# Batch 0 of a fused attention and mixer kernel: keys transposed raw and normed by the scale of the exp, v loaded straight into place, u made by columns in PSUM, the casts of U and V planned later

## The chip, the cores and the metric

The kernel runs on one core of a Trainium2 chip. The metric is the device time of one execution in microseconds, from the runtime; the span of the profile (first to last instruction) is about 1.8 us shorter. Each run lists the mean granted clock of TensorE (1.0 is full speed). Engines: PE is TensorE, DVE VectorE, ACT ScalarE, POOL GpSimd (here it issues the loads), SP SyncE.

## The reference

```python
# q, k, v: [8, 12, 448, 64] float32, tau = 0.1; U [448, 32], V [32, 448], w_ch1 [768, 3072], w_ch2 [3072, 768]
q_n = q / (np.linalg.norm(q, axis=-1, keepdims=True) + 1e-06)
k_n = k / (np.linalg.norm(k, axis=-1, keepdims=True) + 1e-06)
scores = np.matmul(q_n, k_n.transpose(0, 1, 3, 2)) / tau
...                                     # softmax
attn_out = np.matmul(attn, v)
x = attn_out.transpose(0, 2, 1, 3).reshape(8, 448, 768)
h = x.transpose(0, 2, 1) @ U @ V        # low-rank mixing along the sequence
u = x + h.transpose(0, 2, 1)
out = u + np.maximum(u @ w_ch1, 0.0) @ w_ch2
```

Per batch there are thus 12 heads of attention, a small product with U and V, and an MLP of 768 to 3072 to 768. The MLP is most of the arithmetic.

## The kernel before

The order in which each engine issues its instructions isn't written by hand. Every instruction is an `Op` with an estimated duration, dependencies, buffers taken and given back, and a priority; a list scheduler inside the kernel simulates the engines with these estimates and fixes one order for each engine. On the chip each engine then works through its fixed order, whatever the real durations are. One of the estimates is the latency of the loads of U and V (`lat`).

```python
        ld = Slot(r_ld, 3 * (h1 - h0) // 2)
        ops = [load(lambda i=i, src=src: nc.gpsimd.dma_start(
            out=ld.tile[:, i, 0:h1 - h0, :],
            in_=src[b, h0:h1].rearrange("h (s c) d -> s h (c d)", c=SC)),
            (h1 - h0) * 0.5, acq=[ld], late=2.0 if b == 0 else LATE) for i, src in enumerate((q, k))]
        return ld, ops

...

    def load_v0(h0, h1):

        o = load(lambda: nc.gpsimd.dma_start(
            out=v_raw()[:, h0:h1, :], in_=v[0, h0:h1].rearrange("h (s c) d -> s h (c d)", c=SC)),
            (h1 - h0) * 0.5, acq=[raw])
        c = plan.add(Op("ACT/DVE", any_t(256 * (h1 - h0), 2), None, deps=[o, v0_set], prio=0.35,
                        fast=True))
        c.fn = lambda: copy_op(c, v_first()[:, h0:h1, :, 0:D],
                               v_raw()[:, h0:h1, :].rearrange("p h (c d) -> p h c d", c=SC))
        for h in range(h0, h1):
            got[0, h, "v"] = [c]
...
    # norm(): queries (i == 0) into 4 blocks, keys into 8 blocks padded with zeros, all multiplied by
    # 1/norm on DVE; then 12 transposes on PE in two groups, each copied out of PSUM by ACT or DVE
    ops = [part(1, 0), part(1, 1), part(0, 0)]
...
    # attention(), batch 0: 8 scores of 112 x 448 for a pair of heads; scale of the exp is a constant
                nc.tensor.matmul(out=sc.tile[0:rows_, 0:S], lhsT=kT[:, rows_ * m:rows_ * (m + 1)],
                                 rhs=qkT.tile[:, 8:12, :].rearrange("p c s -> p (c s)"),
                                 start=True, stop=True)
            o = plan.add(Op("PE", pe_t(S), score, deps=qdeps, acq=[sc], rel=[qkT]), pe_sc)
            exps[m] = plan.add(Op("ACT", act_t(S), lambda sc=sc, m=m: nc.scalar.activation(
                out=attn.tile[0:rows_, m, off:off + S], in_=sc.tile[0:rows_, 0:S], func=AF.Exp,
                scale=inv_tau), deps=[o], acq=[attn], rel=[sc], prio=0.1 if b == 0 else 1))
...
    # stage0(): A = U^T X (copied out), u = V^T A + X by rows, added on DVE (u_nat), then transposed
    # into uT and copied once more
...
    def cast_v():
        nc.scalar.copy(out=V_sb[:, PAD:PAD + S].rearrange("r (c s) -> r s c", c=SC),
                       in_=V_f().rearrange("r (s c) -> r s c", c=SC))
```

The comments that begin with a name and a colon stand in for cut code.

Of the kernel before, what the change touches and what calls it, by code (L numbers as in the profile page):

```python
# [20 lines left out]
PAD = 64  # L21
# [179 lines left out]
def kernel(  # L201
# [57 lines left out]
    r_inv = ring(3, [SCH, 2, G, SC], FP, "inv")  # L259
# [7 lines left out]
    VN = H * SC * D  # L267
    r_w2 = Ring(1, lambda i: pool.tile([128, VN + H * SC * (D + 2)], BF, name="raw_v", tag="w2", bufs=1)
# [6 lines left out]
    def v_raw():  # L275
        return raw.tile[0:SCH, 0:VN].rearrange("p (h e) -> p h e", h=H)

    def v_first():
        return raw.tile[0:SCH, VN:].rearrange("p (h c d) -> p h c d", h=H, c=SC)

# [15 lines left out]
    ident = const.tile([128, 128], BF, name="ident")  # L296
    w1_sb = const.tile([128, CC, F], BF, name="w1_sb")
# [16 lines left out]
    pe_tp = plan.stream("PE")  # L314
    pe_av = plan.stream("PE")
    pe_a = plan.stream("PE")
    pe_sc = plan.stream("PE")
    pe_mlp = plan.stream("PE")
# [36 lines left out]
    def flip(stream, ins, n, into, part, deps, acq, rel):  # L355
# [3 lines left out]
        for z, x in enumerate(ins):  # L359
            def fn(z=z, x=x):  # L360
                if z == 0:
                    tp.tile = psum.tile([128, len(ins), n], BF, name="tp", tag="mm", bufs=3)
                nc.tensor.transpose(out=tp.tile[:, z, :], in_=x(), identity=ident[:n, :n])  # L363
            o = plan.add(Op("PE", 0.05, fn, deps=deps + [id_set] if z == 0 else (), acq=[tp] + acq,
                            rel=rel if z == len(ins) - 1 else []), stream)
        c = plan.add(Op("ACT/DVE", any_t(n * len(ins), 2), None, deps=[o], acq=acq, rel=[tp],
# [8 lines left out]
    def load_qk(b, h0, h1):  # L375
        ld = Slot(r_ld, 3 * (h1 - h0) // 2)
        ops = [load(lambda i=i, src=src: nc.gpsimd.dma_start(  # L377
            out=ld.tile[:, i, 0:h1 - h0, :],
            in_=src[b, h0:h1].rearrange("h (s c) d -> s h (c d)", c=SC)),
            (h1 - h0) * 0.5, acq=[ld], late=2.0 if b == 0 else LATE) for i, src in enumerate((q, k))]  # L380
        return ld, ops
# [24 lines left out]
    def load_v0(h0, h1):  # L406

        o = load(lambda: nc.gpsimd.dma_start(
            out=v_raw()[:, h0:h1, :], in_=v[0, h0:h1].rearrange("h (s c) d -> s h (c d)", c=SC)),
            (h1 - h0) * 0.5, acq=[raw])  # L410
        c = plan.add(Op("ACT/DVE", any_t(256 * (h1 - h0), 2), None, deps=[o, v0_set], prio=0.35,
                        fast=True))
        c.fn = lambda: copy_op(c, v_first()[:, h0:h1, :, 0:D],
                               v_raw()[:, h0:h1, :].rearrange("p h (c d) -> p h c d", c=SC))
        for h in range(h0, h1):
            got[0, h, "v"] = [c]

    def stats(b, h0, h1, ld, ops):
# [3 lines left out]
        ss, ln, nv, inv = Slot(r_ss, 1), Slot(r_ln, 1), Slot(r_ln, 1), Slot(r_inv, 3 * g // 2)  # L422
        red = []
        for i in range(2):
            for a0 in range(0, g, G // 2):
                a1 = min(g, a0 + G // 2)
                sq = Slot(r_sq, 1)
                o = Op("ACT/DVE" if b == 0 else "DVE", any_t(256 * (a1 - a0), 2, 0.17), None,
                       deps=[ops[i]], acq=[sq], prio=pr + 0.2, fast=True)

                def square(o=o, i=i, a0=a0, a1=a1, sq=sq):
                    x, y = ld.tile[:, i, a0:a1, :], sq.tile[:, 0:a1 - a0, :]
# [18 lines left out]
        o = plan.add(Op("DVE", 0.21, lambda: nc.vector.tensor_scalar_add(  # L451
            nv.tile[:, :, 0:g, :], nv.tile[:, :, 0:g, :], EPS), deps=[o], prio=pr))
        o = plan.add(Op("DVE", 0.35, lambda: nc.vector.reciprocal(
            inv.tile[:, :, 0:g, :], nv.tile[:, :, 0:g, :]), deps=[o], acq=[inv], rel=[nv], prio=pr))
        for p in range(h0 // 2, h1 // 2):
            norm(b, p, ld, inv, 2 * p - h0, [o], pr)

    count = [0]

    def norm(b, p, ld, inv, a, deps, pr):  # L460
# [3 lines left out]
        xn, qkT = Slot(r_xn, 2 if by_pe else 1), Slot(r_qkT, 8 if b == 0 else 7)  # L464
# [31 lines left out]
    def attention(b, p, X):  # L496
        off = PAD * (b % 2)
        qkT, qdeps = got.pop((b, p, "qkT"))
# [4 lines left out]
        for m in range(8 if small else 7):  # L503
            sc = Slot(r_sc, 1)

            def score(sc=sc, m=m):
                kT = qkT.tile[:, 0:8, :].rearrange("p b s -> p (b s)")
                nc.tensor.matmul(out=sc.tile[0:rows_, 0:S], lhsT=kT[:, rows_ * m:rows_ * (m + 1)],  # L508
                                 rhs=qkT.tile[:, 8:12, :].rearrange("p c s -> p (c s)"),
# [324 lines left out]
```

## Time and profile before

| | before |
|---|---|
| time, median of 4 runs | 612.28 us (612.0 to 612.3) |
| span of the profile | 610.5 us |
| first exp of batch 0 | 16.59 us |
| last exp of batch 0 ends | 44.92 us |
| first matmul of the MLP of batch 0 | 48.05 us |
| transposes of batch 1 | 61.05 us |

The lines of the page and the timeline that carry this are in the prediction below. From the first MLP matmul on, PE is dense. So two numbers say almost everything of a version of this kernel: when the MLP starts, and how much of PE's time after that isn't work. I call the second slack: the length of a stretch minus the matmuls in it, each counted by the step at which it follows its neighbour in dense rows (0.1625 us for 384 columns, 0.2155 for 512, 0.19 for a score, 0.032 for an av matmul, 0.05 for a transpose of 112). In the kernel before, the slack is 0.6 us from 60 to 80 us, 1.5 from 80 to 160, and within the error of the count after that, up to the start of the last matmul (3.8 us before the end, in before and after alike).

### The profile page before, as it was taken

Reading aid. Unit: us, or ns where it says so; the run is one execution under the profiler, and the core shown is the slowest. Engines: PE = TensorE matmul, PEld = TensorE weight load, DVE = VectorE, ACT = ScalarE, POOL = GpSimd, SP = SyncE. Lnnn points to the kernel's source line nnn. Section 1 sums busy time; section 2 is a strip of 40 time slices with the busy share of each in tenths; the row PEclk is TensorE's granted clock in tenths of the full one; section 3 lists DMA queues with packets and bytes.
Section 4 is the critical chain, followed back from the end, with each engine's and each line's share of the span. In section 5 each row is a group of like instructions: output and inputs, shape, how many; then the busy total and the mean of one; then the engine's idle time right before and its main releaser. Section 6 shows DMA issues by size and latency. Waiting matters only on the chain.

```text
span 610.5 us, 11561 instructions
## 1 busy us (share of the span) xinstructions
PE 585.5 (96%) x4704; PEld 348.3 (57%) x4728; DVE 298.6 (49%) x758; ACT 285.0 (47%) x609; POOL 109.9 (18%) x168
## 2 busy tenths in 40 slices
PE   0899999999999999999999999999999999999997
PEld 0565666555555665666445666666545666654465
DVE  6977859989999799654820253014300210110011
ACT  4984981288774187407642067505542015014300
POOL 6227160135340627000600000000000000000000
PEclk9999999999999999999999999999999999999999
DMA  9999992999999999644962132031002110410011
GB/s 136 202 204 136 210 156 23 166 138 138 132 125 155 139 185 159 94 84 83 121 37 53 53 72 59 1 84 35 14 1 52 52 40 1 79 52 1 0 53 53
DMA packets 146037, 54.58 MB, mean 89 GB/s; under 512 B 109568, under 2 KB 145984, under 8 KB 145984
## 3 DMA queue, kind: packets, MB, share of 16 engines
q0 software_dynamic: 69216, 25.96, 37.9%
q1 hardware_dynamic: 76704, 27.86, 24.5%
q8 instruction: 37, 0.61, 0.4%
q14 instruction: 16, 0.13, 0.1%
q10 hardware_dynamic: 64, 0.02, 0.0%
HBM read 52.25 MB, written 11.01 MB: 104 GB/s over the span
## 4 chain that ended last, share of the span: by engine, by line
PE 91%; ACT 4%; DVE 2%; SPq 1%; DMA 1%; issue 1%; ACTq 0%
PE mm L670 36%; PE mm L649 35%; PE sc L508 9%; PE av L526 7%; ACT attn L512 3%; PE mm L587 1%; DMA raw_uv<-in_moe_U_dram 1%; PE tp L363 1%; SPq L733 1%; PE mm L559 1%; DVE ss L440 1%; ACT qkT L700 0%; ACT sq L434 0%; ACT uT L700 0%; SPq L763 0%
## 5 line engine op out<-in xcount | busy, mean ns | idle before, releaser
L649 PE MATMUL mm<-uT,w_sb 128*128 128x384 bf16 (+1 forms) x1130 | 235.4, 352 | 0.9
L670 PE MATMUL mm<-w_sb,relu 128*128 128x384 bf16 (+1 forms) x1368 | 233.7, 323 | 0.3 <-ACT uT L700 0.3
L512 ACT ACTIVATE attn<-sc 128x448 bf16<-128x448 f32 (+1 forms) x342 | 165.1, 557 | 91.4 <-PE av L526 57.6
L670 PEld LDWEIGHTS <-relu 128*128 128x128 bf16 x1368 | 132.5, 98 | 87.1 <-issue 1.3
L649 PEld LDWEIGHTS <-w_sb 128*128 128x128 bf16 x1152 | 112.2, 98 | 101.1 <-issue 0.2
L659 ACT ACTIVATE relu<-mm 128x384 bf16<-128x384 f32 (+1 forms) x174 | 95.0, 546 | 150.4 <-PE mm L649 148.6
L679 DVE TENSOR_TENSOR O_sb<-mm,u_nat 128x384 f32<-128x384 f32 (+1 forms) x57 | 31.1, 549 | 231.1 <-PE mm L670 227.6
L508 PE MATMUL sc<-qkT 128*128 128x448 bf16 (+1 forms) x342 | 103.5, 359 | 7.8 <-DVE qkT L702 4.1
L526 PEld LDWEIGHTS <-attn 128*128 128x128 bf16 (+1 forms) x1536 | 61.1, 98 | 16.1 <-issue 2.2
L399 POOL DMA_DIRECT2D v_nat<-in_v_dram x98 | 63.3, 651 | 21.2 <-DMA w_sb<-in_moe_w_ch_dram 5.3
L440 DVE TENSOR_REDUCE ss<-sq 112x8 f32<-112x512 bf16 x96 | 62.9, 672 | 0.5 <-ACT sq L434 0.3
L526 PE MATMUL av<-v_nat,attn 128*128 128x65 bf16 x1344 | 55.6, 193 | 0.0
L377 POOL DMA_DIRECT2D qk_nat<-in_q_dram x25 | 17.8, 713 | 172.3 <-DVE xn L474 115.9
L508 PEld LDWEIGHTS <-qkT 128*128 128x128 bf16 (+1 forms) x342 | 31.3, 104 | 26.0 <-issue 5.8
L535 DVE TENSOR_TENSOR X_sb<-av,rd 128x256 bf16<-128x256 f32 x96 | 40.2, 419 | 1.6
L477 DVE TENSOR_TENSOR xn<-qk_nat,inv 112x256 bf16<-112x256 bf16 x96 | 36.8, 415 | 1.9 <-DMA qkT<-xn 1.8
L533 DVE RECIPROCAL rd<-av 128x4 f32<-128x4 f32 x96 | 17.0, 179 | 34.7 <-PE av L526 33.6
L436 DVE TENSOR_TENSOR sq<-qk_nat 112x512 bf16<-112x512 bf16 x85 | 32.8, 412 | 0.0
L474 DVE TENSOR_TENSOR xn<-qk_nat,inv 112x512 bf16<-112x512 bf16 x48 | 32.6, 680 | 0.0
L601 DVE TENSOR_TENSOR u_nat<-mm,X_sb 128x384 bf16<-128x384 f32 (+2 forms) x45 | 22.4, 527 | 12.7 <-PE mm L587 12.0
L363 PE MATMUL tp<-ident,xn 112*128 112x112 bf16 x144 | 11.2, 226 | 10.4 <-DVE xn L477 10.4
L445 ACT ACTIVATE ln<-ss 112x32 f32<-112x32 f32 (+1 forms) x25 | 6.2, 248 | 31.9 <-DVE ss L440 31.9
(51 smaller groups left out, 175.4 us busy)
## 6 DMA issues: line engine op xcount, KB each, us to landing
qk_nat<-in_q_dram POOLq DMA_DIRECT2D x23, 224.0 KB, 5.7
qk_nat<-in_k_dram POOLq DMA_DIRECT2D x23, 224.0 KB, 6.8
w_sb<-in_moe_w_ch_dram POOLq DMA_DIRECT2D x4, 1152.0 KB, 18.7
w_sb<-in_moe_w_ch_dram POOLq DMA_DIRECT2D x8, 576.0 KB, 14.1
out_dram<-O_sb SPq DMA_DIRECT2D x15, 168.0 KB, 2.2
out_dram<-O_sb SPq DMA_DIRECT2D x16, 144.0 KB, 2.1
out_dram<-O_sb SPq DMA_DIRECT2D x16, 120.0 KB, 1.9
out_dram<-O_sb SPq DMA_DIRECT2D x16, 96.0 KB, 2.2
```

What stands on the lines that cost most here:

```text
L399: nc.gpsimd.dma_start(out=vb[p0:p0 + s1 - s0, hs, j, 0:D], in_=v[b, hs].rearrange("h (s c) d -> c s h d", c=SC)[c, s0:s1]),
L436: nc.vector.tensor_mul(y, x, x)
L440: lambda i=i, a0=a0, a1=a1, sq=sq: nc.vector.reduce_sum(ss.tile[:, i, a0:a1, :].rearrange("p h c -> p (h c)"), sq.tile[:, 0:a1 - a0, :].re ...
L474: nc.vector.tensor_mul(dst, src, sc.to_broadcast([SCH, 2, SC, D]))
L477: nc.vector.tensor_mul(dst, src[:, hh], sc[:, hh].to_broadcast([SCH, SC, D]))
L508: nc.tensor.matmul(out=sc.tile[0:rows_, 0:S], lhsT=kT[:, rows_ * m:rows_ * (m + 1)], rhs=qkT.tile[:, 8:12, :].rearrange("p c s -> p (c s)" ...
L512: exps[m] = plan.add(Op("ACT", act_t(S), lambda sc=sc, m=m: nc.scalar.activation(out=attn.tile[0:rows_, m, off:off + S], in_=sc.tile[0:row ...
L526: nc.tensor.matmul(out=av.tile[:, t, 0:D + 1], lhsT=attn.tile[0:rows_, m, 128 * t:128 * (t + 1)], rhs=vv[0:rows_, h, j, 0:D + 1], start=(j ...
L535: muls.append(plan.add(Op("DVE", dve_t(256), lambda av=av, rd=rd, h=h: nc.vector.tensor_mul(X.tile[:, :, h * D:(h + 1) * D], av.tile[:, :, ...
L649: o = plan.add(Op("PE", pe_t(n), lambda f=f, cc=cc, mm=mm: nc.tensor.matmul(out=mm.tile[:, 0:n], lhsT=w1_sb[:, cc, f * 128:(f + 1) * 128], ...
L659: nc.scalar.activation(out=relu.tile[:, f, 0:n], in_=mm.tile[:, 0:n], func=AF.Relu)
L670: nc.tensor.matmul(out=mm.tile[:, 0:c1 - c0], lhsT=relu.tile[:, f, i * 128:(i + 1) * 128], rhs=w2.tile[:, f, c0:c1], start=(f == 0), stop= ...
```

## The change

The intent is to take work off the path that leads to the first MLP matmul. Keys of batch 0 are transposed as loaded; their norm is multiplied in by the exp, whose scale becomes a per-partition pointer. So that a score has one head's keys in its rows, the queries carry the zero padding (8 blocks) and the keys have 4. tau goes into the norms through a small tile. v is loaded straight into its place by 12 loads in runs of 64 elements, in place of 2 loads and 2 copies. u comes by columns: X is brought in by identity matmuls and V·A added in the same PSUM bank, so one copy makes uT; u by rows is made later. The casts of U and V are planned with a latency of 12 us instead of 2.5, and V's cast writes contiguously. With these come smaller moves: the squares of the later pairs and nearly all copies of batch 0's keys and queries go to DVE, the loads of batch 0 are split and ordered anew, and its scores and the late u by rows get their own place in PE's order.

The core of the diff (ring sizes, renames and the fills of the tau tile are cut):

```diff
+        ops = [load(lambda c=c: nc.gpsimd.dma_start(
+            out=v_first()[:, h0:h1, c, 0:D],
+            in_=v[0, h0:h1].rearrange("h (s c) d -> c s h d", c=SC)[c]),
+            (h1 - h0) * 0.22, deps=[v0_set], acq=[raw]) for c in range(SC)]
...
+    def norm_q(p, ld, ops, la, inv, a, o, pr):
+
+
+        xn, qkT = Slot(r_xn, 1), Slot(r_qkT, 8)
+        EV = "DVE" if p else "ACT/DVE"
+        done = [flip(pe_tp, [(lambda c=c, hh=hh: ld.tile[:, 1, la + hh, c * D:(c + 1) * D])
+                             for c in range(SC) for hh in range(2)],
+                     SCH, lambda: qkT.tile, (lambda t_, x: (t_[:, 8:12, :], x)), [ops[1]], [qkT], [ld], 2, EV)]
+        us = []
+        for hh in range(2):
+            def unit(hh=hh):
+                src = ld.tile[:, 0, la + hh, :].rearrange("p (c d) -> p c d", d=D)
+                nc.vector.tensor_mul(xn.tile[:, 4 * hh:4 * hh + 4, 64 * hh:64 * hh + 64], src,
+                                     inv.tile[:, 0, a + hh, :].unsqueeze(2).to_broadcast([SCH, SC, D]))
+            us.append(plan.add(Op("DVE", dve_t(256), unit, deps=[o, xn_set[count[0] % len(xn_t)]], acq=[xn],
+                                  rel=[ld, inv] if hh else [], prio=pr)))
+        count[0] += 1
+        done.append(flip(pe_tp, [(lambda z=z: xn.tile[:, z, :]) for z in range(8)], SCH,
+                         lambda: qkT.tile, (lambda t_, x: (t_[:, 0:8, :], x)), us, [qkT], [xn], 1, EV))
+        got[0, p, "qkT"] = (qkT, done, inv, a)
...
+                x = qkT.tile
+                if small:
+                    kT, qT = x[:, 8 + m % 4, :], x[:, m // 4 * 4:m // 4 * 4 + 4, :]
+                else:
+                    kT = x[:, 0:8, :].rearrange("p b s -> p (b s)")[:, 128 * m:128 * (m + 1)]
+                    qT = x[:, 8:12, :]
+                nc.tensor.matmul(out=sc.tile[0:rows_, 0:S], lhsT=kT, rhs=qT.rearrange("p c s -> p (c s)"),
                                  start=True, stop=True)
-            o = plan.add(Op("PE", pe_t(S), score, deps=qdeps, acq=[sc], rel=[qkT]), pe_sc)
-            exps[m] = plan.add(Op("ACT", act_t(S), lambda sc=sc, m=m: nc.scalar.activation(
-                out=attn.tile[0:rows_, m, off:off + S], in_=sc.tile[0:rows_, 0:S], func=AF.Exp,
-                scale=inv_tau), deps=[o], acq=[attn], rel=[sc], prio=0.1 if b == 0 else 1))
+
+            def exp(sc=sc, m=m):
+                scale = inv_tau
+                if small:
+                    inv, a = keys
+                    scale = inv.tile[:, 1, a + m // 4, m % 4:m % 4 + 1]
+                nc.scalar.activation(out=attn.tile[0:rows_, m, off:off + S], in_=sc.tile[0:rows_, 0:S],
+                                     func=AF.Exp, scale=scale)
+            o = plan.add(Op("PE", pe_t(S), score, deps=qdeps, acq=[sc], rel=[qkT]), pe_first if small else pe_sc)
+            exps[m] = plan.add(Op("ACT", act_t(S), exp, deps=[o], acq=[attn],
+                                  rel=[sc] + keys[:1], prio=0.1 if b == 0 else 1))
...
+    def columns(X, A, uT, muls, cc, a):
+
+        c0 = 128 * cc
+        mm = Slot(r_mm, 1)
+        st = pe_a if cc < CC - 1 else pe_av
+        X.uses += 1
+        X.left += 1
+        A.uses += 1
+        A.left += 1
+        for t in range(3):
+            plan.add(Op("PE", 0.055, lambda t=t: nc.tensor.matmul(
+                out=mm.tile[:, 128 * t:128 * (t + 1)], lhsT=X.tile[:, t, c0:c0 + 128], rhs=ident,
+                start=(t == 0), stop=False, skip_group_check=True),
+                deps=muls[2 * cc:2 * cc + 2] + [id_set] if t == 0 else (), acq=[mm, uT] if t == 0 else [],
+                rel=[X] if t == 2 else []), st)
+        o = plan.add(Op("PE", pe_t(384), lambda: nc.tensor.matmul(
+            out=mm.tile[:, 0:384], lhsT=A.tile[:, c0:c0 + 128], rhs=V_sb[:, PAD:PAD + 384],
+            start=False, stop=True, skip_group_check=True), deps=[a], rel=[A]), st)
+        c = plan.add(Op("ACT/DVE", any_t(384), None, deps=[o], rel=[mm], prio=0))
+        c.fn = lambda: copy_op(c, uT.tile[:, cc, 0:384], mm.tile[:, 0:384])
+        return c
...
-                    deps=[zf], prio=-2, lat=2.5)))
+                    deps=[zf], prio=-2, lat=12.0)))
...
-        nc.scalar.copy(out=V_sb[:, PAD:PAD + S].rearrange("r (c s) -> r s c", c=SC),
-                       in_=V_f().rearrange("r (s c) -> r s c", c=SC))
+        nc.scalar.copy(out=V_sb[:, PAD:PAD + S].rearrange("r (c s) -> r c s", c=SC),
+                       in_=V_f().rearrange("r (s c) -> r c s", c=SC))
```

## The prediction

> **What bounds the kernel now.** I read the page first, for which engine is full and when.
>
> ```profile
> span 610.5 us, 11561 instructions
> PE 585.5 (96%) x4704; PEld 348.3 (57%) x4728; DVE 298.6 (49%) x758; ACT 285.0 (47%) x609; POOL 109.9 (18%) x168
> PE   0899999999999999999999999999999999999997
> ACT  4984981288774187407642067505542015014300
> ```
>
> PE is full in all slices but the first two and the last; ACT and DVE are full only early. So after the start the kernel is bound by PE, and a change to batch 0 can gain only in the first slices. The timeline (start, duration, engine, line, tile, count) shows what happens there:
>
> ```profile
> 10.41 1.49 PE L363 MATMUL tp<-ident,xn 112*128 112x112 bf16 x12 [10.41 <-DVE xn L477]
> 11.39 2.18 ACT L742 CAST V_sb<-raw_uv 128x448 bf16<-128x448 f32 x1 [1.73 <-DMA raw_uv<-in_moe_V_dram]
> ...
> 16.02 1.28 PE L508 MATMUL sc<-qkT 128*112 128x448 bf16 x3 [4.12 <-DVE qkT L702]
> ...
> 16.59 1.41 ACT L512 ACTIVATE attn<-sc 112x448 bf16<-112x448 f32 x3
> ...
> 30.41 3.69 ACT L512 ACTIVATE attn<-sc 112x448 bf16<-112x448 f32 x8
> ...
> 43.51 1.41 ACT L512 ACTIVATE attn<-sc 112x448 bf16<-112x448 f32 x3 [0.77 <-PE sc L508]
> ...
> 48.05 13.16 PE L649 MATMUL mm<-uT,w_sb 128*128 128x384 bf16 x80
> ```
>
> PE does nothing for 10.4 us, transposes, then waits 4.1 us, because ACT stood at the cast of V (1.7 us for its transfer, 2.2 us of work, then 0.6 us for a transfer of U) with the logarithm of the second norm behind it. From 16.59 to 44.92 ACT runs the 48 exps of batch 0 among 5 squares, 4 copies of keys or queries, norms and copies of A. Table of windows: between 16 and 45 us ACT is busy 27.63 of 29.00. After the last exp 3.1 us of tail lead to the first MLP matmul at 48.05.
>
> From there on I ask how much of PE's time is real work. In dense rows the starts lie 0.1625 us apart for 384 columns (80 matmuls in 13.16), 0.19 for a score, 0.032 for an av matmul, 0.05 for a transpose, 0.2155 for 512 columns. Counts by these steps give about 552 us of work in the 562.4 us from 48.05 to the end: 10 us of slack, of which about 3 lie at the very end, and 2.6 between 61 and 121 us. So the end moves with the start of the MLP of batch 0, minus whatever new holes appear on PE.
>
> **What the Trainium skill says.**
> "TensorE: Matmul & The Clock Gate", Back-to-back issue gap: N/2.4 + 2.5 ns for an isolated warm gap, which makes 162.5 ns for 384 columns. The trace agrees (0.1625 us). The 326 ns that the groups show for one such matmul is latency, which "Perfetto Trace Analysis", Identifying the Most-Contended Engine, warns of: busy time of matmuls is a poor measure. Hence the count above.
> "ScalarE: Activation LUTs", What ACT_TABLE_LOAD costs: an ACTIVATE with immediate scale and bias takes 186 ns + 0.833 ns per element, each per-partition pointer operand adds about 93 ns, neighbours overlap by about 93 ns. For 448 that is 559 alone and 466 apart; the trace has 540 alone and 440 to 450 apart (eight in 3.69 us). The exps of before thus cost as those with immediates. After the change their scale is a pointer into the norms; no run yet shows what that costs here.
> "DMA: Bandwidth & Descriptors", Why small descriptors are slow: a fixed cost per packet and per descriptor. The trace agrees in direction: 12 to 48 us moves up to 214 GB/s, while the loads of v in runs of 64 elements at 48 to 52 us move 88.
>
> **The change part by part.**
>
> *Start.* Keys are transposed raw, so only queries wait for the norm. But the order listing shows DVE doing four sums (both pairs) before the first reciprocal. The fills of DVE end at 7.15 now, two small ones for tau are added: 7.3. Four sums, partly waiting for squares on ACT: to 10.0. Scale 0.17, reciprocal 0.25: 10.5. Two query products at 0.38: 11.3. Eight transposes on a PE that has just begun: 12.0. Copy of 896 by ACT, 0.85: 12.9. Score: first exp about 13.4, against 16.59. Most of these 3.2 us come from the casts of U and V, which are planned with a latency of 12 us instead of 2.5 and now stand after the 16th exp at the latest, where their data has long landed.
>
> *ACT through batch 0.* It loses the 5 squares in this stretch (DVE does them), the 4 copies, and the copy of v (1.29, ahead of the first exp). It keeps 48 exps: 47 steps of 0.44 is 21; with an estimated 0.093 each from the skill's page for the pointer, 4.5 more. Two pairs of ln and exp for norms 0.9, casts of U 0.6, cast of V about 1.0 (its order is changed to contiguous writes; 2.2 before). Sum 28.0. I add 0.9 for a hole between the third and fourth exp, where PE's order has 16 transposes. The last exp ends near 42.3, against 44.92.
>
> *DVE.* Per pair it saves the query product of 0.60 and a copy of v, and takes over squares and all copies of keys and queries but two. Walking its order with the steps of the trace (sum 0.59, product 0.34, copy 0.53 or 0.30, square 0.34) has the third pair's queries ready at 24.3 and the fifth's at 32; ACT reaches them at about 24.6 and 33.5. Close, but ACT stays the slower.
>
> *Tail.* u by columns: the identity matmuls that bring X in can run early; after A only a 384-column matmul and one copy remain instead of product, add, transposes, copy. Saves about 0.5 of 3.1. The MLP starts at 42.3 + 2.6 = 44.9: **3.1 us earlier**.
>
> *PE's added work* lies before this and beside ACT: 16 half or whole transposes per pair instead of 12, 18 identity matmuls for 18 transposes, six matmuls of 384 more: 6 x (4 x 0.05) + 6 x 0.16 = 2.2 us, hidden.
>
> *After.* The order of before puts 80 MLP matmuls, then transposes of batch 1, then its scores with MLP matmuls between all of them. The order of after puts 140 (22.8 us) ahead, so the transposes of batch 1 stand at 44.9 + 22.8 = 67.7 (61.05 now), and the fill is used up: 2 scores, 12 transposes, 10 scores, 12, 2, 12, 2 follow nearly bare. There ACT sets the pace: 14 exps, three copies of 896 at 0.85, norms 1.0. Walking it, from the first transpose to the second av group takes 15 us, with 10.6 us of PE work in it: a **new hole of about 4.2 us**. Against it, the 2.6 us of slack that before has between 61 and 121 are partly filled, since 72 matmuls of the second layer are spread over the rest of batch 1 and 38 of the next MLP come ahead of batch 2: give back 1.5.
>
> Sum: 612.3 - 3.1 + 4.2 - 1.5 = 611.9. If the pointer scale costs nothing, the start moves by another 4 us (607.9). I give that one chance in four, and come to **610.9**.
>
> **The rivals.**
> (1) The early start is kept whole. For it: the plan itself sees 60 more MLP matmuls before batch 1, 9.75 us. Then the second hole eats 2 to 4 of them: 603 to 606. Against it: the plan's exps are 0.427 us, the trace has 0.44 to 0.45, and the pointer isn't in the plan at all.
> (2) Transfers become the bound. v of batch 0 is now 12 loads in runs of 64 elements (two before); at 88 GB/s its 0.69 MB take 7.8 us instead of 3.3. In the trace the first-layer weights land up to 25.8 us after issue, the last at 41.5, and the second-layer ones at 80. All would move by 2 to 4 us. But the last first-layer piece is needed only at 62, and the second layer begins at about 78 with pieces that landed from 61 on. I expect nothing; if a queue wait appears, 614 to 617.
> (3) DVE becomes the bound of batch 0 with the squares it takes over. ACT would then show holes waiting for scores: 1 to 3 us later, 612 to 614.
>
> **Range and chances.** The start is uncertain by 2 us (pointer, cast of V, holes), the hole after it by 1.5, the give-back by 1: together about 2.8, and 1.3 times that, 3.7, on each side: 607.0 to 614.5. A gain of 2% needs 600.0, more than the whole wait before 16 us could return after the hole: 0.02. A loss of 2% needs 624.5: 0.02. Within: 0.96.
>
> **What would show it.** First exp at 13 to 14 us; steps between exps of batch 0 of 0.53 instead of 0.44; the first MLP matmul at 43.5 to 46; 140 MLP matmuls with no gap; then PE waiting for exps and copies between about 67 and 80 us; second-layer matmuls waiting for no transfer. I am wrong if exps keep 0.44 apart and the MLP starts before 42, or if the weights hold PE up.

## More of the kernel before

One pair of rows of before is needed for comparison later. Timeline of DVE before the norms of batch 1 (start, duration, engine, line, operation and tiles, count, and in brackets the idle time before it with what ended it):

```profile
52.91 0.68 DVE L440 TENSOR_REDUCE ss<-sq 112x8 f32<-112x512 bf16 x1
56.95 0.24 DVE L451 TENSOR_SCALAR ln<-ln 112x32 f32<-112x32 f32 x1 [3.37 <-ACT ln L448]
```

DVE has the sums of batch 1's squares and waits 3.37 us for the logarithm, which stands in ACT's order behind the relus of the MLP.

## The result

The changed kernel takes 613.88 us (median of 4 runs, 613.85 to 614.49) against 612.28. The ratio is 1.003, with a 95% interval of 1.0012 to 1.0047. The result is correct.

So it is slower by 1.6 us, where 1.4 faster had been predicted; both lie within 2%, and 613.88 lies within the range.

The page of the kernel after, same lines as those of before in the prediction:

```profile
span 612.7 us, 11615 instructions
PE 590.0 (96%) x4732; PEld 350.2 (57%) x4755; DVE 294.4 (48%) x755; ACT 286.2 (47%) x605; POOL 116.5 (19%) x178
PE   3899899999999999999999999999999999999997
ACT  4985764277874487407742067505542014114300
```

One slice is 15.3 us. The first digit of PE rose from 0 to 3: PE starts earlier. But the fifth digit is now 8 instead of 9: something is lost between 61 and 77 us.

The start. Timeline of ACT after:

```profile
13.20 1.68 ACT L552 ACTIVATE attn<-sc,inv 112x448 bf16<-112x448 f32 x3 [0.62 <-PE sc L544]
15.76 3.25 ACT L552 ACTIVATE attn<-sc,inv 112x448 bf16<-112x448 f32 x6 [0.88 <-PE sc L544]
...
22.93 1.07 ACT L813 CAST V_sb<-raw_uv 128x448 bf16<-128x448 f32 x1
...
31.83 10.07 ACT L552 ACTIVATE attn<-sc,inv 112x448 bf16<-112x448 f32 x19 [0.27 <-PE sc L544]
```

The first exp comes at 13.20 instead of 16.59, V is cast in 1.07 us at 22.93 instead of 2.18 at 11.39, and the last of the 48 exps ends at 31.83 + 10.07 = 41.90 instead of 44.92. Three exps take 1.68 us, where the three of before took 1.41: the pointer costs 0.09 each.

What follows. Timeline of PE after:

```profile
45.03 22.91 PE L720 MATMUL mm<-uT,w_sb 128*128 128x384 bf16 x140
67.78 0.56 PE L364 MATMUL tp<-ident,xn 112*128 112x112 bf16 x8
...
69.77 0.54 PE L544 MATMUL sc<-qkT 128*128 128x448 bf16 x2 [0.58 <-ACT qkT L771]
70.15 0.75 PE L364 MATMUL tp<-ident,xn 112*128 112x112 bf16 x12
...
72.26 3.57 PE L544 MATMUL sc<-qkT 128*128 128x448 bf16 x8 [0.98 <-ACT attn L552]
75.62 1.32 PE L364 MATMUL tp<-ident,xn 112*128 112x112 bf16 x12
```

The MLP starts 3.0 us earlier. 140 matmuls run without a gap, and then there is nothing to put between the scores of batch 1: eight of them take 3.57 us, 0.43 apart instead of 0.19, because each waits for a buffer that an exp gives back. Between 67.78 and 82.23 the steps above give 9.5 us of work in 14.45: some 4.9 lost (4.6 in the count of the table below).

Why do 140 matmuls stand ahead of batch 1? Timelines of ACT and DVE after, at the norms of batch 1:

```profile
50.69 0.68 DVE L440 TENSOR_REDUCE ss<-sq 112x8 f32<-112x512 bf16 x1
63.69 0.18 DVE L454 TENSOR_SCALAR ln<-ln 112x32 f32<-112x32 f32 x1 [12.31 <-ACT ln L448]
```

```profile
62.78 0.49 ACT L730 ACTIVATE relu<-mm 128x384 bf16<-128x384 f32 x1 [0.48 <-PE mm L720]
63.17 0.22 ACT L445 ACTIVATE ln<-ss 112x32 f32<-112x32 f32 x1
63.42 0.23 ACT L448 ACTIVATE ln<-ln 112x32 f32<-112x32 f32 x1
```

The squares and sums of batch 1 are done early, so its data was there. But DVE then stands for 12.31 us (3.37 before), since ACT has the logarithm behind a row of relus that are paced by the MLP, 0.975 us apart. The chip wasn't late; the plan's estimate of the loads of batch 1 was.

A last reading from the table of windows of after (columns: stretch, its length; busy time and count of PE, PEld, DVE, ACT, POOL; then granted clock, DMA share, GB/s):

```profile
65.00:70.00 5.00, 4.42 (x37) 2.83 (x35) 4.23 (x10) 3.04 (x6) 1.45 (x2) 1.00 1.16 210
70.00:75.00 5.00, 3.60 (x23) 1.51 (x22) 5.00 (x14) 4.84 (x12) 0.00 (x0) 0.95 1.16 210
75.00:80.00 5.00, 5.00 (x64) 3.72 (x63) 3.10 (x9) 4.60 (x11) 1.40 (x2) 0.71 1.16 210
```

In this run the clock was cut to half behind the thin stretch, for 3.4 us from 74.5 us on (a window from 74.52 to 77.92 shows 0.50; the 0.95 and 0.71 above are means over 5 us). The twelve transposes at 75.62 take 1.32 us, those at 70.15 only 0.75. The three other runs of this kernel have a mean clock of 1.0 and spans of 612.1, so the cut probably cost 0.6 us of the 4.6.

### The profile page after: what moved, and what is told of

The parts are those of the page before. It is cut to its first block, busy times and chain, and to the rows that moved or that the text cites. A ratio compares the mean times of both kernels' runs of the same rounds, so it can differ in the third digit from the quotient of the medians.

```text
span 612.7 us, 11615 instructions
## 1 busy us (share of the span) xinstructions
PE 590.0 (96%) x4732; PEld 350.2 (57%) x4755; DVE 294.4 (48%) x755; ACT 286.2 (47%) x605; POOL 116.5 (19%) x178
## 4 chain that ended last, share of the span: by engine, by line
PE 91%; DVE 4%; ACT 4%; issue 1%; ACTq 0%
PE mm L720 35%; PE mm L741 34%; PE sc L544 10%; PE av L568 7%; ACT attn L552 3%; PE tp L364 1%; PE mm L657 1%; DVE ss L440 1%; PE mm L625 1%; DVE u_nat L671 1%; ACT qkT L771 1%; DVE O_sb L750 0%; DVE xn L482 0%; DVE xn L776 0%; DVE xn L508 0%
## 5 line engine op out<-in xcount | busy, mean ns | idle before, releaser
L741 PE MATMUL mm<-w_sb,relu 128*128 128x384 bf16 (+1 forms) x1368 | 238.0, 323 | 0.2 <-DVE O_sb L750 0.2
L720 PE MATMUL mm<-uT,w_sb 128*128 128x384 bf16 (+1 forms) x1130 | 228.5, 352 | 0.8
L552 ACT ACTIVATE attn<-sc 128x448 bf16<-128x448 f32 x294 | 140.9, 550 | 81.2 <-PE av L568 51.5
L730 ACT ACTIVATE relu<-mm 128x384 bf16<-128x384 f32 (+1 forms) x179 | 97.3, 544 | 154.4 <-PE mm L720 154.3
L436 DVE TENSOR_TENSOR sq<-qk_nat 112x512 bf16<-112x512 bf16 x92 | 35.6, 413 | 0.0
L508 DVE TENSOR_TENSOR xn<-qk_nat,inv 112x256 bf16<-112x256 bf16 x84 | 32.5, 412 | 0.4 <-DMA qkT<-xn 0.3
L505 DVE TENSOR_TENSOR xn<-qk_nat,inv 112x512 bf16<-112x512 bf16 x42 | 28.8, 686 | 0.0
L552 ACT ACTIVATE attn<-sc,inv 112x448 bf16<-112x448 f32 x48 | 26.3, 675 | 2.0 <-PE sc L544 2.0
L671 DVE TENSOR_TENSOR u_nat<-mm,X_sb 128x384 bf16<-128x384 f32 x36 | 19.2, 551 | 10.0 <-PE mm L657 10.0
L380 POOL DMA_DIRECT2D qk_nat<-in_k_dram x25 | 17.6, 703 | 2.1 <-PE sc L544 2.0
```

The source lines that it names most:

```text
L380: ops = [load(lambda i=i, src=src: nc.gpsimd.dma_start(out=ld.tile[:, i, lo:lo + h1 - h0, :], in_=src[b, h0:h1].rearrange("h (s c) d -> s ...
L436: nc.vector.tensor_mul(y, x, x)
L508: nc.vector.tensor_mul(dst, src[:, hh], sc[:, hh].to_broadcast([SCH, SC, D]))
L552: nc.scalar.activation(out=attn.tile[0:rows_, m, off:off + S], in_=sc.tile[0:rows_, 0:S], func=AF.Exp, scale=scale)
L720: o = plan.add(Op("PE", pe_t(n), lambda f=f, cc=cc, mm=mm: nc.tensor.matmul(out=mm.tile[:, 0:n], lhsT=w1_sb[:, cc, f * 128:(f + 1) * 128], ...
L730: nc.scalar.activation(out=relu.tile[:, f, 0:n], in_=mm.tile[:, 0:n], func=AF.Relu)
```

## The experiments

Twelve kernels ran, each in five rounds beside the kernel before (e34 has six runs, e6 four). The runs of before that each group shares have medians of 612.26, 612.17, 612.33 and 612.26. This table has all of it. "Ahead" is the number of MLP matmuls of batch 0 that stand in PE's order before the transposes of batch 1; "start" is the first MLP matmul; the slacks are as defined above; all from the profiled run of each kernel.

| kernel | ahead | start | slack 60-80 | slack 80-160 | start + slack | span | span minus that | median us |
|---|---|---|---|---|---|---|---|---|
| before | 80 | 48.05 | 0.6 | 1.5 | 50.2 | 610.5 | 560.3 | 612.28 |
| after | 140 | 45.03 | 4.6 | 3.2 | 52.8 | 612.7 | 559.9 | 613.88 |
| e1_imm (wrong result) | 140 | 42.70 | 3.9 | 2.9 | 49.5 | 610.2 | 560.7 | 612.07 |
| e2_late | 103 | 45.03 | 0.7 | 2.9 | 48.6 | 608.8 | 560.2 | 610.60 |
| e12_both (wrong result) | 103 | 43.38 | 0.8 | 2.7 | 46.9 | 607.1 | 560.2 | 608.67 |
| e3_casts | 72 | 46.60 | -0.1 | 1.7 | 48.2 | 608.8 | 560.6 | 610.10 |
| e34_casts_late | 36 | 46.11 | 0.0 | 3.2 | 49.4 | 609.3 | 559.9 | 611.96 |
| e25_vraw_late | 62 | 46.81 | 0.8 | 2.2 | 49.8 | 610.1 | 560.3 | 611.95 |
| e5_vraw | 99 | 46.68 | 0.3 | 2.5 | 49.5 | 610.4 | 560.9 | 612.22 |
| e6_nocol | 121 | 46.87 | 0.8 | 7.0 | 54.6 | 616.9 | 562.3 | 617.59 |
| e7_normed | 132 | 44.02 | 2.7 | 3.0 | 49.7 | 610.3 | 560.6 | 612.26 |
| e7_normed_late | 95 | 44.26 | 1.1 | 1.9 | 47.3 | 607.8 | 560.5 | 609.41 |
| e4_before_late | 45 | 48.15 | 0.4 | 4.7 | 53.2 | 613.4 | 560.2 | 615.18 |
| e8_half | 121 | 45.07 | 2.1 | 3.3 | 50.5 | 610.7 | 560.2 | 612.44 |

The second column from the right is the test of the reading: for 13 of 14 kernels the span is 560.4 us plus the start plus the slack from 60 to 160 us, within 0.5. So the start and the slack explain the times, and nothing else of that size does. The one that falls out, e6, lost 1.4 us between 46.87 and 60, ahead of the stretch counted, to 3.4 us at half clock (its 121 matmuls take 21.10 us from the first start to the next row, where 121 x 0.1625 is 19.66).

Read differences between kernels here, not single slacks. A recount from the same traces gives 0.2 to 0.4 us more from 60 to 80 and 0.8 to 1.4 us more from 80 to 160 in every kernel, since steps of some small matmuls have to be chosen and some records are missing. It moves the constant to 558.4 to 559.4 (561.0 in e6). PE's work after the start is 553.4 to 553.8 us in all fourteen.

My theory after the first comparison: the start gained 3 us as predicted; the place of batch 1 in the order, set by a wrong estimate of its loads, makes the hole; the pointer scale eats part of what raw keys save. Rivals: a hole set by the exps and copies of batch 1 whatever the order; the 12 short-run loads of v; and u by columns.

### e1_imm: the exps of batch 0 with a constant scale

Wrong: the keys' norms are replaced by one number.

```diff
-                    scale = inv.tile[:, 1, a + m // 4, m % 4:m % 4 + 1]
+                    scale = inv_tau / 0.8
```

> The changed kernel with the scale of the 48 exps of batch 0 as one number (10/0.8, wrong on purpose: keys are then not normed) instead of a pointer to the norms; order of instructions unchanged. My theory: the pointer costs about 0.085 us per exp and ACT is the bound of batch 0. Then exps lie 0.44 apart instead of 0.525, the first MLP matmul moves from 45.0 to 41.0 to 42.5 us, the 140 matmuls and the hole behind them stay as they are, and the time falls from 613.9 to 610 to 611.5. Rival: DVE or PE set the pace of batch 0 and ACT would only wait more; MLP start above 44, time above 613.

Measured: relative error 0.0945; 612.07 us (612.0 to 612.97), ratio to before 1.0005 (0.9993 to 1.0018). Timeline of ACT in e1:

```profile
13.20 1.41 ACT L552 ACTIVATE attn<-sc 112x448 bf16<-112x448 f32 x3 [0.62 <-PE sc L544]
15.76 2.71 ACT L552 ACTIVATE attn<-sc 112x448 bf16<-112x448 f32 x6 [1.15 <-PE sc L544]
...
23.77 2.28 ACT L552 ACTIVATE attn<-sc 112x448 bf16<-112x448 f32 x5 [0.73 <-PE sc L544]
...
30.36 8.77 ACT L552 ACTIVATE attn<-sc 112x448 bf16<-112x448 f32 x19 [0.54 <-PE sc L544]
```

The order is that of the changed kernel, so rows can be compared one to one: 1.68 against 1.41 for three, 3.25 against 2.71 for six, 10.07 against 8.77 for nineteen. The pointer costs 0.09, 0.09 and 0.07 us an exp, some 3.8 us over 48. The MLP start moved by 2.3 of these (42.70): the waits for scores grew (1.15 from 0.88, 0.73 from 0.21, 0.54 from 0.27), because PE and DVE can't feed a faster ACT. That start is just later than the theory's 42.5 at most, and the time misses 611.5 by 0.6: 1.8 us gained over the changed kernel. The hole stayed, at 3.9.

### e2_late: keys and queries of batch 1 planned 6 us earlier

```diff
-            (h1 - h0) * 0.5, acq=[ld], late=2.0 if b == 0 else LATE) for i, src in enumerate((q, k))]
+            (h1 - h0) * 0.5, acq=[ld], late=2.0 if b < 2 else LATE) for i, src in enumerate((q, k))]
```

The work stays the same; the plan's order changes, and with it the engine of two jobs that ACT or DVE may take (605 and 755 instructions in the changed kernel, 603 and 757 in e2).

> The changed kernel with one number of its plan changed: queries and keys of batch 1 are planned to land 6 us earlier, so that the order puts 103 instead of 140 MLP matmuls ahead of their transposes and fills the scores with the rest. My theory: the order, not the data, makes the hole; MLP start stays at 45.0, transposes of batch 1 at about 62, the 4.6 us of lost PE time after them fall below 1.5, time 609.5 to 611.5. Rival: the plan was right and the data is late; PE or DVE waits for a transfer and the time stays at 613 or more.

Measured: correct, 610.6 us (610.55 to 610.87), ratio to before 0.9976 (0.9964 to 0.9989). Timeline of PE in e2:

```profile
45.03 16.90 PE L720 MATMUL mm<-uT,w_sb 128*128 128x384 bf16 x103
61.77 0.56 PE L364 MATMUL tp<-ident,xn 112*128 112x112 bf16 x8
...
66.77 0.35 PE L544 MATMUL sc<-qkT 128*128 128x448 bf16 x1
66.96 0.49 PE L720 MATMUL mm<-uT,w_sb 128*128 128x384 bf16 x2
```

Same start to the hundredth, and the hole is gone (0.7 us): between the scores there are MLP matmuls again. One estimate is worth 3.3 us. The norms of batch 1 were ready in time for the earlier place, so the rival that exps and copies make the hole whatever the order falls too.

### e12_both: the two together

The edits of e1 and e2, so wrong.

> Both edits together (wrong on purpose as the first). If both costs are real and separate they add: MLP start at 41 to 42.5 and no hole, 606.5 to 608.5. If the hole only moves with the start (the data of batch 1 lands near 46 us whatever PE does), less: 609 to 610.5.

Measured: 608.67 us (608.24 to 608.91), ratio 0.9944 (0.9931 to 0.9956), just above the range. The MLP starts at 43.38, past the 41 to 42.5 expected and not at 42.70 as in e1: the plan is another one. The parts nearly add (1.8 and 3.3 alone, 5.2 together).

### e3_casts: only the casts, in the kernel before

```diff
-                    deps=[zf], prio=-2, lat=2.5)))
+                    deps=[zf], prio=-2, lat=12.0)))
...
-                      acq=[uv], prio=-2, lat=2.5)) for t in range(4)]
+                      acq=[uv], prio=-2, lat=12.0)) for t in range(4)]
...
-        nc.scalar.copy(out=V_sb[:, PAD:PAD + S].rearrange("r (c s) -> r s c", c=SC),
-                       in_=V_f().rearrange("r (s c) -> r s c", c=SC))
+        nc.scalar.copy(out=V_sb[:, PAD:PAD + S].rearrange("r (c s) -> r c s", c=SC),
+                       in_=V_f().rearrange("r (s c) -> r c s", c=SC))
...
-              plan.add(Op("ACT", 0.5, cast_v, deps=v0 + [z], rel=[uv], prio=3)),
+              plan.add(Op("ACT", 1.0, cast_v, deps=v0 + [z], rel=[uv], prio=3)),
```

> The kernel before with only the casts of U and V changed as in the change (planned for 12 us instead of 2.5, V written contiguously). My theory: most of the earlier first exp comes from these casts; first exp at 13.3 to 14.2 instead of 16.6, then ACT still has its squares and copies, MLP start at 46 to 47.2, time 610.5 to 612. Rival: the raw keys bring the start; then the first exp stays above 15 and the time at 612.3.

Measured: correct, 610.1 us (609.88 to 610.68), ratio 0.9968 (0.9955 to 0.9982). Timeline of ACT in e3:

```profile
13.18 1.41 ACT L512 ACTIVATE attn<-sc 112x448 bf16<-112x448 f32 x3 [0.37 <-PE sc L508]
...
21.54 1.06 ACT L742 CAST V_sb<-raw_uv 128x448 bf16<-128x448 f32 x1
```

Slightly better than expected. The casts alone bring the first exp from 16.59 to 13.18; the whole change brings it no further (13.20). Two edits are in this run, the later place and the contiguous writes. V's cast now stands behind the first exp, at 21.54, so its faster write (1.06 us instead of 2.18) can't be what brought that exp forward; what it gives later wasn't tried alone. Of the 3.4 us, 1.45 arrive at the MLP start (46.60), since ACT still has its squares and copies. And with 72 matmuls ahead there is no hole, so this small part of the change beats both the kernel before (by 2.2 us) and the whole change (by 3.8).

### e34_casts_late: both planning edits in the kernel before

The edits of e3 and of e2.

> The kernel before with the casts of e3 and with keys and queries of batch 1 planned 6 us earlier as in e2; correct result. Its order puts 36 matmuls of the MLP ahead of the transposes of batch 1 (72 in e3). Theory (the place of batch 1 relative to the MLP decides whether there is a hole, and e3 has none at 72 matmuls): moving batch 1 still earlier gains nothing more; the time stays at 609.5 to 610.8, MLP start 46 to 47. Rival (every microsecond of earlier batch 1 helps, because more MLP matmuls are left to fill the waits of batch 2 and later): 608 to 609.3. Against both: if 36 matmuls are too few to cover the logarithm, norms and copies of batch 1, a hole of 1 to 2 us appears before its first transposes, 611 to 612.

Measured: correct, 611.96 us (611.16 to 614.31), ratio 1.0006 (0.9991 to 1.0022). The theory said 609.5 to 610.8, so this missed. The start moved on to 46.11, but the slack after 80 us rose from 1.7 to 3.2. With only 36 matmuls ahead of batch 1, the MLP's later matmuls are spent among the scores, and waits appear further on (argued; the slack wasn't traced wait by wait). The time lies in the range of the third forecast, but the hole that it named, ahead of the first transposes, isn't there: the 36 matmuls run from 46.11 to 52.05 without one. The six runs also spread with the clock: spans of 609.4 and 609.6 at a mean clock of 1.0, 610.7 at 0.996, 611.7 at 0.994, 612.5 at 0.993. At full clock e34 is 1.3 us slower than e3 (608.1), not 1.9.

### e4_before_late: the planning edit alone, in the kernel before

The edit of e2.

> The kernel before with keys and queries of batch 1 planned 6 us earlier and nothing else; correct result; 45 matmuls ahead of the transposes of batch 1 instead of 80. Control: before has no hole there (0.6 us of slack between 60 and 80 us), so the planning alone has nothing to give. Theory: 612 to 614, as e34 against e3 (1.9 us slower by the medians). Rival (the planning helps by itself, and e2 owes its gain to it rather than to the hole of the changed kernel): 610.5 or less.

Measured: correct, 615.18 us (614.81 to 615.28), ratio 1.0044 (1.0031 to 1.0057). The direction is the theory's, the size above its range: 2.9 us slower. The slack from 80 to 160 us went from 1.5 to 4.7. More than half of that rise is one wait behind the tail of batch 1. Timeline of PE in e4:

```profile
120.58 0.35 PE L508 MATMUL sc<-qkT 128*128 128x448 bf16 x1 [1.67 <-ACT attn L512]
```

So planning batch 1 early isn't good in itself; it is good where too many MLP matmuls stood ahead, bad where there were about enough. The rival (e2 owes its gain to the planning alone) is refuted.

### e8_half: half of e2's shift

```diff
-            (h1 - h0) * 0.5, acq=[ld], late=2.0 if b == 0 else LATE) for i, src in enumerate((q, k))]
+            (h1 - h0) * 0.5, acq=[ld], late=2.0 if b == 0 else 5.0 if b == 1 else LATE) for i, src in enumerate((q, k))]
```

> The changed kernel with keys and queries of batch 1 planned 3 us earlier, half of what e2 does; correct result. 121 matmuls ahead of the transposes of batch 1 (140 in the changed kernel, 103 in e2). Theory (the hole grows with the fill that was used up before it): MLP start 45.03 as in both, slack on PE from 60 to 80 us between their 4.6 and 0.7, at 1.5 to 3.0; time between 610.9 and 612.8. Rival (a threshold: any fill left among the first scores closes the hole): slack under 1.0 and time as e2, 610.3 to 610.9. Rival (e2 gained from something else than the place of batch 1): 613 or more.

Measured: correct, 612.44 us (612.43 to 612.74), ratio 1.0003 (0.9989 to 1.0016). Ahead 103, 121, 140: slack from 60 to 80 us 0.7, 2.1, 4.6; time 610.6, 612.44, 613.88. The start was the same within 0.04 us. That is a dose and its response, inside the theory's ranges: in this plan the hole grows with the fill used up ahead of it. The count ahead doesn't fix it for every plan: e6 below also has 121, and a slack of 0.8.

### e5_vraw and e25_vraw_late: v loaded whole and copied

```diff
-        ops = [load(lambda c=c: nc.gpsimd.dma_start(
-            out=v_first()[:, h0:h1, c, 0:D],
-            in_=v[0, h0:h1].rearrange("h (s c) d -> c s h d", c=SC)[c]),
-            (h1 - h0) * 0.22, deps=[v0_set], acq=[raw]) for c in range(SC)]
-        for h in range(h0, h1):
-            got[0, h, "v"] = ops
+        o = load(lambda: nc.gpsimd.dma_start(
+            out=v_raw()[:, h0:h1, :], in_=v[0, h0:h1].rearrange("h (s c) d -> s h (c d)", c=SC)),
+            (h1 - h0) * 0.5, acq=[raw])
+        c = plan.add(Op("ACT/DVE", any_t(256 * (h1 - h0), 2), None, deps=[o, v0_set], prio=0.35,
+                        fast=True))
+        c.fn = lambda: copy_op(c, v_first()[:, h0:h1, :, 0:D],
+                               v_raw()[:, h0:h1, :].rearrange("p h (c d) -> p h c d", c=SC))
+        for h in range(h0, h1):
+            got[0, h, "v"] = [c]
```

> The changed kernel with v of batch 0 loaded whole in 3 loads and copied into place, as before, and nothing else changed; correct result. Its order puts 99 matmuls ahead of the transposes of batch 1 (140 in the changed kernel). Theory (the hole after the fill is the cost): the transposes of batch 1 stand near 61 to 62, the hole shrinks from 4.6 to under 1.5 us, time 610 to 611.5. Rival (the hole is made by the copies and exps of batch 1 themselves and stays whatever the order): 613 to 614.5.

> The changed kernel with the planning of e2 and with v of batch 0 loaded whole in 3 loads and copied into place, as before; correct result. 62 matmuls of the MLP stand ahead of the transposes of batch 1 (140 in the changed kernel, 103 in e2). Theory (order decides, the loads of v in short runs cost nothing that ends up on the path): as e2, 610.0 to 611.2, MLP start 44.5 to 46.0 because three copies of v return to DVE or ACT. Rival 2 of the prediction (the 12 short-run loads of v push later transfers): e25 is faster than e2 by 1 us or more, 608 to 609.5.

Measured: e5 is correct at 612.22 us (612.07 to 612.49), ratio 1.0002 (0.999 to 1.0013); e25 is correct at 611.95 us (611.71 to 612.2), ratio 0.9996 (0.9984 to 1.0008). Timeline of ACT in e5:

```profile
23.81 1.13 ACT L778 COPY raw_v<-raw_v 112x1024 bf16<-112x1024 bf16 x1
...
30.86 12.69 ACT L559 ACTIVATE attn<-sc,inv 112x448 bf16<-112x448 f32 x24 [0.37 <-PE sc L551]
```

A copy of v is back on ACT, and the last exp ends at 43.55, 1.65 us later than in the changed kernel; the MLP start follows (46.68). The hole shrinks to 0.3 us because the new plan puts 99 matmuls ahead, not 140. For e5 the hole part of the theory held (under 1.5), while the time is 0.7 us above its range, and e25 is 0.8 us above its range in start and in time: I had not counted on the later start. e25 against e2 (62 and 103 ahead, both without a hole) is 1.35 us slower (1.1 between their runs at full clock, spans of 609.9 and 608.8). So v straight into place gains 1.65 to 1.8 us at the start. As a whole e5 is 1.7 us faster than the changed kernel, but by its other order: the hole fell by 4.3. Where neither has a hole, the kernel without the short-run loads is the slower one, so the rival that forecast e25 at 1 us or more below e2 is refuted.

### e6_nocol: u as before

```diff
-            if b == 0:
-                ut += [columns(X, A, uT, muls, cc, a) for cc in range(c0 // 128, c1 // 128)]
...
-        late = b == 0
+        late = False
```

(The buffer count and the priority of the adds go back with it.)

> The changed kernel with u made as before (product, add, transposes, copy) and nothing else undone; correct result. 121 matmuls ahead of the transposes of batch 1. Theory: the tail to the MLP is longer by the predicted 0.5 us, so the MLP starts at 45.4 to 46.0 instead of 45.03; the hole is 19 matmuls (3.1 us) earlier and smaller, 2 to 4 us; and the 12 products of V and A that the change adds late are gone from PE (about 1.5 us). Time 611 to 613. Rival (u by columns pays more than 0.5 us): MLP start after 46.5 and time 614 or more.

Measured: correct, 617.59 us (616.97 to 618.67), ratio 1.009 (1.0077 to 1.0103). The theory missed: both numbers of the rival hold (MLP start after 46.5, 614 or more), and the hole from 60 to 80 us, expected at 2 to 4, is 0.8. From the last exp to the MLP start it takes 4.68 us (42.19 to 46.87) instead of 3.13 in the changed kernel. But that is half of the loss at most. The rest is a hole of another place. Timeline of PE in e6:

```profile
120.51 0.24 PE L625 MATMUL sc<-X_sb,U_sb 128*32 128x128 bf16 x4 [0.57 <-ACT attn L552]
...
123.10 0.23 PE L655 MATMUL sc<-A_sb,V_sb 128*128 128x128 bf16 x1 [0.46 <-DVE u_nat L666]
124.13 0.55 PE L544 MATMUL sc<-qkT 128*128 128x448 bf16 x2 [0.81 <-DVE u_nat L669]
```

The tail of batch 1 (u by rows) and the scores of batch 2 follow each other with no second-layer matmul left to fill: 5.2 us of slack between 120 and 140. Its four timed runs have clocks of 0.994 to 0.997, and the profile shows two cuts to half clock of 3.4 us, from 46.35 and from 124.86 us, each in or just behind a stretch where PE has holes (0.66 and 0.67 as means over 5 us). So undoing one part re-plans a place 70 us further on. e6 shows that u by columns isn't where the time went; what it is worth by itself can't be read from its total.

### e7_normed and e7_normed_late: raw keys undone

e7 is the changed kernel with keys and queries of batch 0 normed before the transposes, as before, and a constant scale; e7_normed_late has the edit of e2 in addition.

```diff
-            if b == 0:
-                norm_q(p, ld, ops, lo + 2 * p - h0, inv, 2 * p - h0, o, pr)
-            else:
-                norm(b, p, ld, inv, 2 * p - h0, [o], pr)
+            norm(b, p, ld, inv, 2 * p - h0, [o], pr, lo)
...
-                if small:
-                    inv, a = keys
-                    scale = inv.tile[:, 1, a + m // 4, m % 4:m % 4 + 1]
```

> The changed kernel with its first part undone and nothing else: keys and queries of batch 0 both normed before the transposes, exps with an immediate scale; v straight into place, u by columns and the later casts stay. Correct result. 132 matmuls stand ahead of the transposes of batch 1 (140 in the changed kernel). By subtraction of the runs so far, raw keys do not pay: casts took the MLP start from 48.05 to 46.60, undoing v costs 1.65 to 1.8, undoing u by columns 1.84, so casts, v and u alone should give 46.60 - 1.7 - 1.84, about 43.1. Theory (the pointer scale eats all that raw keys save): MLP start 42.8 to 43.8 although the first exp comes later than 13.2; transposes of batch 1 at about 65; the hole stays, 3 to 5 us; time 610.5 to 612.5, faster than the changed kernel by 1.5 to 3. Rival (raw keys pay as intended, the parts do not add): MLP start at 45.5 or later, time 613.5 or more.

> e7 with keys and queries of batch 1 planned 6 us earlier, as in e2; correct result; 95 matmuls ahead of the transposes of batch 1. Theory: the early start without the hole, so MLP start as e7 (within 0.5 us), slack on PE from 60 to 140 us at 3 to 4 instead of 6 to 8, time 608 to 609.5: the fastest correct version. Rival (the hole is not set by the order): within 0.7 us of e7.

Measured: e7 is correct at 612.26 us (612.03 to 613.61), ratio 1.0002 (0.9989 to 1.0016). e7_normed_late is correct at 609.41 us (609.32 to 609.55), ratio 0.9951 (0.9939 to 0.9964). Timeline of ACT in e7:

```profile
13.90 1.41 ACT L543 ACTIVATE attn<-sc 112x448 bf16<-112x448 f32 x3 [1.06 <-PE sc L538]
...
30.66 9.79 ACT L543 ACTIVATE attn<-sc 112x448 bf16<-112x448 f32 x21
```

The first exp comes 0.7 us later than with raw keys, but 21 exps take 9.79 us (0.46 apart against 0.52), the last ends at 40.45, and the MLP starts at 44.02, 1.0 us earlier than in the changed kernel (just outside the 42.8 to 43.8 expected; the hole, 2.7, is just under its range). So with the rest of the change in place raw keys cost time: they bring the first exp forward by 0.7 us and spare products and copies, but the pointer adds 3.8 us (e1) to 48 exps on the engine that bounds this stretch. With the order mended as well, e7_normed_late is the fastest correct version of all: 2.9 us faster than before, 4.5 faster than the changed kernel.

## Why the prediction was right or wrong

**The bound.** Right. PE after the start bounds the kernel; the table's near-constant column shows it for every version.

**The start.** Right in size: 44.9 predicted for the MLP, 45.03 measured; first exp 13.4 and 13.20; last exp 42.3 and 41.90. "Most of these 3.2 us come from the casts" was right and too careful: e3 gives all of them by the casts alone, though raw keys still make 0.7 us of it in the changed kernel (e7).

**The pointer.** Right: 0.093 us each was the estimate, 0.07 to 0.09 measured, 3.8 us over the exps instead of 4.5. The branch "if the pointer scale costs nothing, the start moves by another 4 us (607.9)" failed in the other direction: e1 takes the pointer away and gains 2.3 us of start and 1.8 of time, as waits for scores take the rest.

**The tail.** Wrong. u by columns was to save about 0.5 of 3.1 us between last exp and MLP. It is 3.13 us in both kernels (44.92 to 48.05, 41.90 to 45.03). That the start came out within 0.13 us is luck: the exps ended 0.4 us earlier than predicted, and the tail is 0.5 longer. (In e6, without columns, the tail is 4.68; so columns may have bought back what the new order costs there, which isn't settled.)

**The hole.** Right: 140 matmuls without a gap, transposes of batch 1 at 67.78 (67.7 predicted), then waits for exps and copies; 4.6 us lost in the profiled run, some 0.6 of it by the clock, against 4.2 predicted (before has 0.6 there, so 3.4 to 4.0 of it are new). e2 and e8 show that the order is its cause.

**The give-back.** This step failed, and it is why the sum came out on the wrong side of before. "Give back 1.5" should have come from filling the slack of before. From 80 to 160 us the slack was 1.5 us in before and became 3.2: 1.7 lost (1.4 by the recount), nothing returned. Timeline of PE at the tail of batch 1, before:

```profile
105.43 1.89 PE L363 MATMUL tp<-ident,u_nat 128*128 128x128 bf16 x24 [0.32 <-DVE O_sb L679]
107.60 11.86 PE L670 MATMUL mm<-w_sb,relu 128*128 128x384 bf16 x72 [0.28 <-ACT uT L700]
```

and after:

```profile
97.78 1.80 PE L364 MATMUL tp<-ident,xn 112*128 112x112 bf16 x24 [0.32 <-DVE O_sb L750]
...
114.46 0.61 PE L568 MATMUL av<-v_nat,attn 128*128 128x65 bf16 x14 [0.32 <-ACT attn L552]
...
119.86 0.68 PE L364 MATMUL tp<-ident,u_nat 128*128 128x128 bf16 x3
121.10 0.23 PE L364 MATMUL tp<-ident,u_nat 128*128 128x128 bf16 x1 [0.56 <-DVE u_nat L671]
```

Before had 72 second-layer matmuls in one block right behind 24 transposes of u. After they are spread over batch 1, and the last transposes of u wait for their adds bare. Gap by gap, as time beyond the step, the tail itself is little worse: 1.6 us from 119.4 to 121.4 against 1.3 from 104.8 to 107.6 in before. The rest is ahead of it: 0.8 us around the last 24 transposes of batch 1's keys and queries (97.78), which before had done by 81.5 without a wait, and 0.5 where av matmuls wait for an exp (114.46). e1, e2 and e8 have the same gaps within 0.05 us, whatever their hole (e2 has 2.9 us of slack there), so this isn't a consequence of the hole. Early filler can be missed later in other orders too: e34 and e4 lose 1.5 and 3.2 us after 80 us against e3 and before, for 0.5 at most gained ahead of it.

**The sum by its terms,** with before's 0.6 us between 60 and 80 subtracted: -3.0 for the start, +4.0 for the hole, +1.7 in place of -1.5 gives +2.7; the spans differ by 2.2, and the count is good to about 0.5 (the recount gives +2.4). The predicted terms gave -0.4, lowered to 610.9 by the one chance in four for a free pointer. The range has a small slip: 3.7 on each side of 610.9 is 607.2 to 614.6, not 607.0 to 614.5. The measured time lies in either, 3.0 us above the middle.

**The rivals.** (1) kept whole: refuted, 45.03 and yet slower. (2) transfers: refuted by e25 against e2, and the waits of PE after the start show no transfer. (3) DVE as the bound of batch 0: the changed kernel's holes of ACT are small (0.88 us the longest), but e1 shows that it comes next, with 1.15, 0.73 and 0.54.

What stays open: the slack from 80 to 160 us (1.5 to 4.7 in the kernels other than e6) isn't traced to single waits for every version, nor to one part of the change, and what u by columns is worth by itself isn't settled, as each undoing makes another plan.

## What to carry to other kernels

Where one engine is full, write the time as start plus slack and a constant, and check that the constant holds over the versions; then each edit can be read as a move of one of the two. When an earlier start comes from a plan with estimated durations, look at what the plan puts into the time gained: here it used up the filler that the next stage needed, and one wrong estimate of a load cost more than the start had gained. And moving a product into the scale of an activation isn't free where that activation's engine is the bound: multiply the pointer's cost by the number of activations first.

## What the Trainium skill lacked or had wrong

- "TensorE: Matmul & The Clock Gate", Part 1: The HAM clock gate, has the clock at half rate after an idle window of about 3.4 us. The records here show such half rate (0.50 for 3.4 us from 74.5 us in after), but PE had no gap over 0.98 us in the stretch from 67.78 us; in the 3.4 us just before the cut (71.1 to 74.5) it was busy for 2.00 us with 7 matmuls. e3, e5, e6 and e25 have cuts of 3.4 us too, in or behind stretches where PE was thinly used (0.66 to 0.84 as means over 5 us), while other runs of e3 and e25 have 1.0. The page says that the window is free-running, and elsewhere that frequent short idle times of PE make the clock go back and forth; it lacks what this costs one core at such short gaps. Between runs of one kernel at mean clocks of 0.997 and 1.0 the spans here differ by 0.2 us (610.1 and 609.9 in e25), 0.6 (612.7 and 612.1 in after), 0.9 (611.1 and 610.2 in e1) and 1.5 (611.8 and 610.3 in e7); at 0.993 by 3.1 (612.5 and 609.4 in e34).
- "ScalarE: Activation LUTs", What ACT_TABLE_LOAD costs, has about 93 ns for a pointer operand. The runs agree for short rows of exps (0.09 us each, 1.68 against 1.41 for three) and show less in a long one (0.07 each, 10.07 against 8.77 for nineteen), where the exps without a pointer were themselves slower.
